# Spectral filter loaded in interleaved sets of 32 partitions, with another column order of the row tables

## The chip, the cores and the metric

The kernel runs on one core of one Trainium2 chip. The metric is the device time of one launch in microseconds (us). The kernel before takes 358.42 us, the median of three runs that lie between 358.37 and 358.54 us. Its profiled execution spans 357.2 us, and all positions in time below are counted from the start of that span.

## The reference

The program is a forward pass and its gradients. `x` is 2048 x 448 in bfloat16.

```python
def _A_ref(x, w_r, w_i):                      # spectral mixer
    X = rfft2(x.astype(float32), axes=(-2, -1))   # 2048 x 225 complex
    X = X * (w_r + 1j * w_i)
    return irfft2(X, s=(S, D)).astype(bfloat16)

h  = x + _A_ref(layernorm(x), A_w_r, A_w_i)
h2 = h + _B_ref(layernorm(h), w1, b1, w2, b2)  # layernorm, matmul, gelu, matmul over the 2048 axis
_out, _vjp = jax.vjp(f, A_x, A_w_r, A_w_i, B_w1, B_b1, B_w2, B_b2)
return (_out, *_vjp(grad_out))
```

The filter `w_r + i*w_i` has 2048 rows of 225 numbers in each of its two components; a component is 900 KB. It is read once, for the forward product, and its gradient has the same shape and is written as two outputs. What the change touches is only how the filter comes in, in which order its rows lie on the 128 partitions, and how its gradient goes out.

## The kernel before, in words

The 2048-point Fourier transform along the sequence is split into two stages, 128 = 16 x 8 by way of 16-point and 128-point parts. In the *row phase* (the loop `for t in range(NT)` at line 905) TensorE makes the 448-point transforms of the rows and the first stage: `row_a`, `row_b`. Each `row_b` pair ends in a 226 KB transfer from SBUF to SBUF (line 693) that writes 16 partitions of `D2`. There are eight of them. The *second stage* (`s2_stage`, line 696) multiplies all of `D2` by the row tables `Ut` and `Vt`, for 16 groups g of 128 rows each. The first of these products needs all eight transfers, since it contracts over all partitions of `D2`. Then `w_mult` on VectorE multiplies the result with the filter, and `s2_inv` starts the inverse transform. Its results leave by transfers of 113 KB (line 756), each of which writes 8 partitions of `D3`.

The tables `Ut` and `Vt` are made in `gen_UV` (line 465). Their column p decides which row of the spectrum falls on partition p. For the lower 64 partitions p = 4l+f, with l from 0 to 15 and f from 0 to 3. In the upper 64 the kernel before uses two blocks: partitions 64 to 111 for the residues 1 to 3 (stride 3) and 112 to 127 for residue 0 (contiguous). A table is written by eight instructions, each with 256 elements per partition, one per residue j and half; a running load count at build time picks ScalarE or VectorE for each.

The filter rows must lie in the same order. `w_load` (line 579) reads each component with four transfers into `W_rows` (a part of the region rB): 64 partitions, 48 partitions, and 16 partitions in two pieces. `w_place` (line 588) copies `W_rows` into `W_view_F` (region rG), 16 copies on ScalarE and VectorE, the upper half with its order of groups turned round. The copies are called from `s2_stage` from its fourth step (c2 = 3) on. The gradient of the filter leaves late in the kernel through `w_io` (line 563), eight transfers that `gx_consumer` (line 1358) starts at the steps named in `GW_AT`.

All engines that matter follow an order written out by hand: TensorE, VectorE, ScalarE and SyncE run their instructions in the order in which the program names them. Nearly all transfers are issued by SyncE on one queue (q1). Each takes the next of eight semaphores, so a transfer also waits until the one eight places before it has landed.

In the row phase SyncE issues, among others, the transfers to `D2`, the transposed loads of `B_w2` (`load_w2T`, line 292, 512 KB each) and the first component of the filter, one call of `w_loads` at each of the steps t = 9, 10, 11, 12. At the first step of the second stage the string `"TWWWWTTT"` (line 946) gives the order: one transposed load (T), the four loads of the second component (W), then the other transposed loads. The transposed loads feed `dg_gen` (line 827), a long product of 14 blocks of 16 matmuls with `B_w2`. `fill(n)` puts n of these matmuls between the steps of the other phases, so that TensorE has something to do there. In the second stage three stand after each half step. Block j of `dg_gen` can't start before its transposed load has landed, and since TensorE keeps its order, the second stage waits with it.

Of the kernel before, what the change touches and what calls it, by code (L numbers as in the profile page):

```python
# [17 lines left out]
P = 128  # L18
S = 2048
D = 448  # L20
DF = 225
# [101 lines left out]
def kernel(  # L123
# [20 lines left out]
    nc = tc.nc  # L144
# [110 lines left out]
    def col(n=1):  # L255
        i = _ci[0]
        _ci[0] += n
        assert _ci[0] <= 64
        return cols[:, i:i + n]
# [69 lines left out]
    def ftmp(off, *dims):  # L329
        n = int(np.prod(dims))  # L330
        v = tf[:, off:off + n]
        if len(dims) == 1:
            return v
        names = "abcd"[:len(dims)]
        return v.rearrange("p (" + " ".join(names) + ") -> p " + " ".join(names),
                           **{c: d for c, d in zip(names, dims)})
# [68 lines left out]
    def gp_madd(out, in0, scalar, in1):  # L405
        gp_.tensor_scalar(out=gtmp, in0=in0, scalar1=scalar, scalar2=None, op0=ALU.mult)
        gp_.tensor_tensor(out=out, in0=gtmp, in1=in1, op=ALU.add)
# [34 lines left out]
    def decode(eng):  # L442
        a4, fc, s_, c_, f_ = col(), col(), col(), col(), col()
        floor_div(eng, a4, pcolb, 64)
        gp_madd(s_, a4, -64.0, pcolb)
        floor_div(eng, fc, s_, 8)
        gp_madd(s_, fc, -8.0, s_)
        gp_madd(s_, s_, 2.0, a4)
        floor_div(eng, c_, fc, 4)
        gp_madd(f_, c_, -4.0, fc)  # L450
        return fc, s_, c_, f_
# [13 lines left out]
    def gen_UV():  # L465
        _, s_, c_, f_ = rows = decode(gp_)
        nrow = col()
        gp_madd(nrow, rows[0], 16.0, s_)
        msk, mk, k0, k1 = masks(gp_, c_, f_)
        slf = col()  # L470
        gp_.tensor_tensor(out=slf, in0=s_, in1=f_, op=ALU.mult)
        gp_.tensor_scalar(out=slf, in0=slf, scalar1=16.0, scalar2=1536.0, op0=ALU.mult, op1=ALU.add)
        ou, ov0, ov1, pu, pv = col(), col(), col(), col(), col()
        gp_madd(ou, c_, 1536.0, slf)
        gp_madd(ov0, c_, -512.0, slf)
        gp_.tensor_scalar(out=ov0, in0=ov0, scalar1=512.0, scalar2=None, op0=ALU.add)
        gp_.tensor_scalar(out=ov1, in0=ov0, scalar1=1024.0, scalar2=None, op0=ALU.add)
        for pt, o, kk in ((pu, ou, -1536.0), (pv, ov1, -512.0)):
            gp_.tensor_scalar(out=pt, in0=s_, scalar1=64.0, scalar2=kk, op0=ALU.mult, op1=ALU.add)
            gp_madd(pt, pt, mk, o)  # L480
        yield
        ve.tensor_scalar(out=permI[:], in0=krow[:, 0:P], scalar1=nrow, scalar2=None, op0=ALU.is_equal)
        ve.scalar_tensor_tensor(out=base[:, 0, :, 1], in0=fix, scalar=mk, in1=base[:, 0, :, 1], op0=ALU.mult, op1=ALU.add)
        for dst, o0, o1, pt in ((Ut, ou, ou, pu), (Vt, ov0, ov1, pv)):
            t = ftmp(1024 if dst is Ut else 2048, 16, 16, 2).bitcast(I32)
            for k, o in ((0, o0), (1, o1)):
                ve.tensor_scalar(out=t[:, :, :, k], in0=base[:, :, :, k], scalar1=s_, scalar2=o,
                                 op0=ALU.mult, op1=ALU.add)
                yield
            ve.tensor_scalar(out=t[:, 0, :, 1], in0=base[:, 0, :, 1], scalar1=s_, scalar2=pt, op0=ALU.mult, op1=ALU.add)  # L490
            ve.tensor_scalar(out=t, in0=t, scalar1=2047, scalar2=None, op0=ALU.bitwise_and)
            yield
            yield True
            comp = comp_ring.next()
            sc.activation(out=comp, in_=t.rearrange("p g l c -> p (g l c)"), func=ACT.Sin, scale=s2048, bias=half_uv)
            yield True
            cv = comp.rearrange("p (g l c) -> p g l c", g=16, l=16)
            for c, k in ((1, k0), (0, k1)):
                ve.tensor_scalar(out=cv[:, 0, :, c], in0=cv[:, 0, :, c], scalar1=k, scalar2=None, op0=ALU.mult)
            yield  # L500
            d0 = dst[:, :, 0:64].rearrange("p g (l f) -> p g l f", f=4)
            d1 = dst[:, :, 64:112].rearrange("p g (l f) -> p g l f", f=3)
            for j in range(4):
                m = msk[:, j:j + 1]
                dj = d1[:, :, :, j - 1] if j else dst[:, :, 112:128]
                for o, c in ((d0[:, :, :, j], 0), (dj, 1)):
                    if load[1] + 0.24 < load[0] + 0.38:
                        ve.tensor_scalar(out=o, in0=cv[:, :, :, c], scalar1=m, scalar2=None, op0=ALU.mult)
                    else:
                        sc.activation(out=o, in_=cv[:, :, :, c], func=ACT.Copy, scale=m)  # L510
                    yield
# [50 lines left out]

    def w_io(Wv, dr, di, store):
        for c_, d in ((0, dr), (1, di)):
            for p0, p1, g0, g1, row, dims in ((0, 64, 0, 16, 0, [[16 * DF, 4], [1, 16 * DF]]),
                                              (64, 112, 0, 16, 112, [[-DF, 48], [1, DF]]),
                                              (112, 128, 1, 16, 127, [[-DF, 15], [1, DF]]),
                                              (112, 128, 0, 1, 64, [[1, DF]])):
                sb = Wv[p0:p1, g0:g1, c_, 0:DF]
                d_ap = bass.AP(d.tensor, d.offset + row * DF, [[P * DF, 16]] + dims)  # L570
                if store:
                    nc.sync.dma_start(out=d_ap, in_=sb)
                else:
                    nc.sync.dma_start(out=sb, in_=d_ap)
                yield

    W_rows = cut(rB, 0, 2, NG, DF)

    def w_load():
        for c_, d in ((0, A_w_r), (1, A_w_i)):  # L580
            for p0, p1, j0, j1, row, dims in ((0, 64, 0, 16, 0, [[16 * DF, 4]]), (64, 112, 0, 16, 97, [[-16 * DF, 3]]),
                                              (112, 128, 0, 15, 113, []), (112, 128, 15, 16, 64, [])):
                nc.sync.dma_start(out=W_rows[p0:p1, c_, j0:j1, :],
                                  in_=bass.AP(d.tensor, d.offset + row * DF,
                                              [[P * DF, 16]] + dims + [[1, (j1 - j0) * DF]]))
                yield

    def w_place():
# [316 lines left out]
    for t in range(NT):  # L905
        if t in (1, 3):
            load_w2T()
        if t + 1 < NT:
            row_a(t + 1, Rs.pop(t + 1))
        fill(FILL_A[t])  # L910
        if 1 <= t and t + 3 < NT:
            if t + 3 in (4, 8, 12):
                while Meter.side:
                    Meter.side.pop(0)()
            Rs[t + 3] = scale_R(t + 3)
        row_b(t - 1)
        if t == NT - 1:
            row_b(t)
        if t % 2 and t < 12:
            fold_prep(xn, t // 2 + 2)  # L920
        for i in STATS.get(t, ()):
            ln_stats(xn, i, mvx)
        for _ in range(3 if t > 0 else 0):
            if next(uv, None):
                break
        if t in GROUPS:
            a, b = GROUPS[t]
            newton_gp(mvx[:, a:b, 1], rstd_x[:, a:b], slice(a, b))
        for _ in range((9, 10, 11, 12).count(t)):
            next(w_loads)  # L930
        if t in INV_S:
            gen_inv_s(INV_S[t])
        if t in (13, 13 + 1):
            gen_neg((cut(r448, NG * P, 12, P), cut(rE, 3 * NT * P, 4, P))[t - 13], Ut[:, 12 * (t - 13):12 + 4 * (t - 13), :])
        if t == 2:
            gen_RT()
        fill(FILL_B[t])
# [5 lines left out]

    def fwd_x(c2):
        if c2 == 0:
            for kind in "TWWWWTTT":
                if kind == "W":
                    next(w_loads)
                elif held_w2:
                    held_w2.pop(0)()  # L950
            cap[0] = NFB
            while held_w2:
                held_w2.pop(0)()
        if c2 == 4:
            turn_biases()
        return Xs[:, 2 * c2:2 * c2 + 2, :, :]

    def fwd_mult(c2, xc):
        return w_mult(c2, xc, W_view_F, False)

    s2_stage(fwd_x, fwd_mult, ML_F, 3, 24, True)
    drain()

# [283 lines left out]
    for t in range(NT):  # L1247
# [6 lines left out]
        pb, tmp, m1, m2, _ = ln_a(t, pdh[:, 0:D], rstd_h[:, t:t + 1], hln[:, t, :], (1.0 + LN_EPS) / D)  # L1254
# [98 lines left out]
    Meter.slack = 2.0  # L1353
    g_out = w_io(W_view_B, out_2, out_3, True)
    X_AT = {0: 2, 4: 3}
    GW_AT = (1, 3, 5, 6, 7, 9, 11, 12)

    def gx_consumer(t, py):
        if t in X_AT:
            load_xall(X_AT[t])  # L1360
        if t in GW_AT:
            next(g_out, None)
# [87 lines left out]
```

## Time and profile before

| what | value |
|---|---|
| median time | 358.42 us |
| span of the profiled execution | 357.2 us |
| TensorE matmul busy | 341.5 us (96%) |
| VectorE busy | 252.5 us (71%) |
| ScalarE busy | 213.8 us (60%) |
| transfers on queue q1 | 80.83 MB, 94.7% of 16 engines' span |
| first component issued / landed | 35.61 to 38.67 us / 46.15 us |
| second component issued / landed | 49.55 to 51.90 us / 57.73 us |
| last transfer to D2 issued / landed | 46.63 / 50.01 us |
| transposed load behind the second component, issued / landed | 52.00 / 60.61 us |

Busy time is the sum of an engine's instructions. The chain of work that ended last is followed back from the last instruction to whatever released it, so it tells which engine or transfer held up the end. A transfer's landing is the last of its completion marks: the trace keeps a mark for each DMA engine that finishes its part, and the landing times above are read from those marks.

### The profile page before, as it was taken

The page shows a single profiled execution, that of the slowest core. Times are in us where ns is not written, and L with a number is a line of the kernel's source. Part 1 is how long each engine was busy: PE and PEld are TensorE (multiplying, and loading weights), DVE is VectorE, ACT ScalarE, POOL GpSimd, SP SyncE. Part 2 cuts the span into 40 slices and gives each one's busy share as a digit, 9 for nine tenths or more (in the row PEclk, how much of TensorE's full clock was granted, in tenths as well). Part 3 has the DMA queues.
Part 4 walks back from the last instruction along what each step waited for, and adds up shares of the span by engine and source line. Part 5 has one row for each costly group of instructions (what it writes and reads, how often), then busy time and mean ns, then how long its engine had stood idle before and what let it go on. Part 6 is the DMA issues. An engine that isn't in the chain of part 4 may idle for free.

```text
span 357.2 us, 6450 instructions
## 1 busy us (share of the span) xinstructions
PE 341.5 (96%) x2133; PEld 183.8 (51%) x2133; DVE 252.5 (71%) x679; ACT 213.8 (60%) x457; POOL 67.7 (19%) x227
## 2 busy tenths in 40 slices
PE   6898998899999999999999999999999999999994
PEld 2455665555645555555555555544444444455641
DVE  5897626992884888775226978784498766499994
ACT  4669836965986545504221355565477776588883
POOL 8667000000220000001001111110000000056771
PEclk9699999999999999999999999999999999999998
DMA  8999999847999999997886999999976878999996
GB/s 207 287 200 234 200 198 162 169 140 252 280 292 336 302 348 241 252 246 218 194 192 134 192 210 194 221 175 264 264 214 201 238 196 236 245 215 221 247 286 234
DMA packets 147672, 81.62 MB, mean 229 GB/s; under 512 B 95480, under 2 KB 139768, under 8 KB 147384
## 3 DMA queue, kind: packets, MB, share of 16 engines
q1 hardware_dynamic: 147352, 80.83, 94.7%
q8 instruction: 16, 0.26, 0.3%
q10 hardware_dynamic: 288, 0.39, 0.3%
q14 instruction: 16, 0.13, 0.1%
HBM read 27.56 MB, written 23.89 MB: 144 GB/s over the span
## 4 chain that ended last, share of the span: by engine, by line
PE 79%; ACT 7%; DVE 6%; DMA 4%; issue 2%; SPq 1%; POOL 0%; ACTq 0%; DVEq 0%
PE ps_mm L218 66%; PE ps_ff L218 13%; DMA rO<-in_B_w_dram 2%; ACT rO L82 2%; DVE stats L82 2%; ACT rG L82 1%; DMA rA<-in_A_x_dram 1%; DVE r L82 1%; ACT Ut L82 1%; DVE rA L82 1%; DVE rS L82 1%; SPq L297 1%; ACT Vt L82 1%; ACT rX L82 0%; ACT rS L82 0%
## 5 line engine op out<-in xcount | busy, mean ns | idle before, releaser
L218 PEld LDWEIGHTS <-r 128*128 128x128 bf16 (+2 forms) x660 | 61.7, 104 | 49.6 <-issue 2.7
L218 PEld LDWEIGHTS <-rS 128*128 128x128 bf16 (+2 forms) x496 | 40.5, 99 | 38.3 <-issue 7.0
L218 PE MATMUL ps_mm<-rD,r 128*128 128x448 bf16 x224 | 44.5, 352 | 0.0
L82 ACT CAST rO<-ps_mm 128x512 bf16<-128x512 f32 (+1 forms) x62 | 33.5, 583 | 13.8 <-PE ps_mm L218 11.1
L218 PE MATMUL ps_mm<-rC,rE 128*128 128x448 bf16 x144 | 36.0, 369 | 3.3 <-DMA rC<-in_grad_out_dram 3.3
L218 PEld LDWEIGHTS <-rst 128*128 128x128 bf16 (+1 forms) x320 | 23.8, 97 | 29.3 <-issue 13.5
L82 ACT CAST r<-ps_ff 128x452 bf16<-128x452 f32 x58 | 33.4, 576 | 8.8 <-PE ps_ff L218 8.4
L218 PE MATMUL ps_mm<-r,rst 128*128 128x512 bf16 (+3 forms) x192 | 36.4, 353 | 0.0
L218 PE MATMUL ps_mm<-rB,r 128*128 128x448 bf16 x160 | 31.2, 352 | 0.1
L218 PE MATMUL ps_mm<-rG,rst 128*128 128x512 bf16 (+1 forms) x128 | 28.2, 380 | 0.0
L82 ACT ACTIVATE r<-ps_mm,rstd_h 128x448 bf16<-128x448 f32 x16 | 10.1, 633 | 26.1 <-PE ps_mm L218 26.1
L82 ACT ACTIVATE r<-rC 128x448 bf16<-128x448 bf16 x16 | 9.1, 572 | 26.8 <-DMA out_dram<-r 12.9
L82 DVE SCALAR_TENSOR_TENSOR r<-ps_mm,b2col,r 128x448 bf16<-128x448 f32 x16 | 10.9, 682 | 19.9 <-PE ps_mm L218 17.9
L82 DVE CAST rO<-ps_mm 128x512 bf16<-128x512 f32 (+1 forms) x18 | 11.8, 658 | 15.2 <-PE ps_mm L218 14.3
L82 ACT ACTIVATE rG<-rG 128x896 bf16<-128x896 bf16 x14 | 13.3, 950 | 14.9 <-DVE rG L82 14.6
L218 PEld LDWEIGHTS <-rO 128*128 128x128 bf16 (+1 forms) x165 | 15.6, 98 | 12.2 <-DMA rO<-in_B_w_dram 1.8
L218 PE MATMUL ps_mm<-rE,rS 128*128 128x448 bf16 x112 | 21.5, 352 | 0.0
L82 ACT CAST rG<-ps_mm 128x512 bf16<-128x512 f32 (+1 forms) x33 | 16.6, 541 | 7.3 <-PE ps_mm L218 7.2
L1180 POOL TENSOR_SCALAR lcol<-lcol 128x1 f32<-128x1 f32 x16 | 8.5, 530 | 65.1 <-ACT r L82 65.1
L218 PE MATMUL ps_mm<-rC,rO 128*128 128x448 bf16 x80 | 19.1, 352 | 1.5 <-DMA rO<-in_B_w_dram 1.5
L1371 POOL TENSOR_SCALAR lcol<-lcol 128x1 f32<-128x1 f32 x16 | 5.5, 342 | 78.5 <-ACT r L82 78.5
L218 PEld LDWEIGHTS <-rE 128*128 128x128 bf16 x148 | 14.4, 101 | 11.3 <-issue 5.0
(198 smaller groups left out, 662.6 us busy)
## 6 DMA issues: line engine op xcount, KB each, us to landing
out_dram<-rO SPq DMA_DIRECT2D x34, 256.0 KB
r<-in_B_w_dram SPq DMA_DIRECT2D x5, 1024.0 KB
r<-r SPq DMA_DIRECT2D x16, 226.0 KB
r<-r SPq DMA_DIRECT2D x32, 113.0 KB
rS<-in_B_w_dram SPq DMA_DIRECT2D x4, 896.0 KB
out_dram<-rG SPq DMA_DIRECT2D x10, 256.0 KB
rO<-in_B_w_dram SPq DMA_DIRECT2D x2, 1024.0 KB
w_d<-rG SPq DMA_DIRECT2D x1, 1808.0 KB
```

The source lines that it names most:

```text
L82: fn(**kw)
L218: nc.tensor.matmul(out, lhsT=lhsT, rhs=rhs, start=start, stop=stop)
L297: nc.sync.dma_start_transpose(out=wT, in_=B_w2[j * P:(j + 1) * P, :].rearrange("f (t c) -> f t c", c=P))
L1180: gp_.tensor_scalar(out=m1, in0=ms, scalar1=-1.0 / D, scalar2=None, op0=ALU.mult)
L1371: gp_.tensor_scalar(out=m1, in0=ms, scalar1=-2.0 / D, scalar2=None, op0=ALU.mult)
```

## The change

Each component of the filter now comes in with five transfers in place of four: for each residue b one that takes the partitions b, b+4, b+8, ..., 32 of them, half of them below 64 and half above; residue 0 is cut in two, since its upper rows are shifted by one group. The aim is that a transfer writes into both halves of the partitions. For this the upper half of the tables and of the filter must have the same interleaving as the lower half, p = 64+4l+j, which changes the columns of `Ut` and `Vt` and the row lists of the gradient's store: six transfers per component there, since three sets of 16 partitions take the place of one of 48. The loads of the first component are called at t = 9 (two), 10, 11 and 12, and the second component has five Ws in its string. The twelve stores start at steps 1 to 12.

```diff
@@ gen_UV
             d0 = dst[:, :, 0:64].rearrange("p g (l f) -> p g l f", f=4)
-            d1 = dst[:, :, 64:112].rearrange("p g (l f) -> p g l f", f=3)
+            d1 = dst[:, :, 64:P].rearrange("p g (l f) -> p g l f", f=4)
             for j in range(4):
                 m = msk[:, j:j + 1]
-                dj = d1[:, :, :, j - 1] if j else dst[:, :, 112:128]
-                for o, c in ((d0[:, :, :, j], 0), (dj, 1)):
+                for o, c in ((d0[:, :, :, j], 0), (d1[:, :, :, j], 1)):
@@ w_io
-            for p0, p1, g0, g1, row, dims in ((0, 64, 0, 16, 0, [[16 * DF, 4], [1, 16 * DF]]),
-                                              (64, 112, 0, 16, 112, [[-DF, 48], [1, DF]]),
-                                              (112, 128, 1, 16, 127, [[-DF, 15], [1, DF]]),
-                                              (112, 128, 0, 1, 64, [[1, DF]])):
-                sb = Wv[p0:p1, g0:g1, c_, 0:DF]
+            for sl, g0, g1, row, dims in ((slice(0, 64), 0, 16, 0, [[16 * DF, 4], [1, 16 * DF]]),
+                                          (slice(65, P, 4), 0, 16, 112, [[-DF, 16], [1, DF]]),
+                                          (slice(66, P, 4), 0, 16, 96, [[-DF, 16], [1, DF]]),
+                                          (slice(67, P, 4), 0, 16, 80, [[-DF, 16], [1, DF]]),
+                                          (slice(64, P, 4), 1, 16, 127, [[-DF, 15], [1, DF]]),
+                                          (slice(64, P, 4), 0, 1, 64, [[1, DF]])):
+                sb = Wv[sl, g0:g1, c_, 0:DF]
@@ w_load
-            for p0, p1, j0, j1, row, dims in ((0, 64, 0, 16, 0, [[16 * DF, 4]]), (64, 112, 0, 16, 97, [[-16 * DF, 3]]),
-                                              (112, 128, 0, 15, 113, []), (112, 128, 15, 16, 64, [])):
-                nc.sync.dma_start(out=W_rows[p0:p1, c_, j0:j1, :],
+            for b, j0, j1, row, up in ((0, 0, 15, 0, 113), (0, 15, 16, 15, 49), (1, 0, 16, 16, 81), (2, 0, 16, 32, 49), (3, 0, 16, 48, 17)):
+                nc.sync.dma_start(out=W_rows[b:P:4, c_, j0:j1, :],
                                   in_=bass.AP(d.tensor, d.offset + row * DF,
-                                              [[P * DF, 16]] + dims + [[1, (j1 - j0) * DF]]))
+                                              [[up * DF, 2], [P * DF, 16], [1, (j1 - j0) * DF]]))
@@ row phase, fwd_x, the gradient's store
-        for _ in range((9, 10, 11, 12).count(t)):
+        for _ in range((9, 9, 10, 11, 12).count(t)):
-            for kind in "TWWWWTTT":
+            for kind in "TWWWWWTTT":
-    GW_AT = (1, 3, 5, 6, 7, 9, 11, 12)
+    GW_AT = (1, 2, 3, 4, 5, 6, 7, 8, 9, 10, 11, 12)
```

## The prediction

> **What bounds the kernel now.** I read the page first: what ended last, by engine and line.
>
> ```profile
> PE 79%; ACT 7%; DVE 6%; DMA 4%; issue 2%; SPq 1%; POOL 0%; ACTq 0%; DVEq 0%
> PE ps_mm L218 66%; PE ps_ff L218 13%; DMA rO<-in_B_w_dram 2%; ACT rO L82 2%; DVE stats L82 2%; ACT rG L82 1%; DMA rA<-in_A_x_dram 1%; DVE r L82 1%; ACT Ut L82 1%; DVE rA L82 1%; DVE rS L82 1%; SPq L297 1%; ACT Vt L82 1%; ACT rX L82 0%; ACT rS L82 0%
> ```
>
> TensorE sets the end, so a change counts only where it lengthens or shortens a wait of TensorE. One transfer has 2% of the chain: a transposed load of `B_w2` into rO. The chain between 44 and 64 us shows where.
>
> ```profile
> 45.90 4.35 PE ps_mm L218 x23
> ...
> 52.00 8.60 DMA rO<-in_B_w_dram
> 60.61 0.05 issue
> 60.65 0.55 PE ps_mm L218 x2
> ```
>
> That load is issued at 52.00 and lands at 60.61. Next I took SyncE's order of issue (start, duration, line) to see what stands ahead of it.
>
> ```profile
> 35.61 1.28 SPq L583 DMA_DIRECT2D rB<-in_A_w_r_dram  x2
> ...
> 49.55 2.35 SPq L583 DMA_DIRECT2D rB<-in_A_w_i_dram  x4
> 52.00 5.02 SPq L297 DMA_TRANSPOSE rO<-in_B_w_dram  x1
> ```
>
> Directly ahead of it is the filter's second component (L583). Last, TensorE and VectorE in that stretch:
>
> ```profile
> 50.31 0.35 PE L218 MATMUL ps_ff<-r,Vt 128*128 128x452 bf16 x1
> ...
> 60.65 0.55 PE L218 MATMUL ps_mm<-rC,rO 128*128 128x448 bf16 x2 [1.50 <-DMA rO<-in_B_w_dram]
> ```
> ```profile
> 57.72 2.89 DVE L82 COPY rG<-rB 64x900 bf16<-64x900 bf16 x7
> ```
>
> The second stage begins at 50.31, 0.3 us after the last transfer to D2 lands (50.01). TensorE waits 1.50 us for the transposed load. The filter lands at 57.73, when VectorE copies it. So what delays D2 delays TensorE, the transposed load is late already, and the filter comes just in time. All three run on one queue, q1.
>
> [...] While the 64-partition load runs, 39.50 to 41.50 us, the core moves 194 GB/s; the 128-partition store at 86.50 to 90.00 gives 355 GB/s. In the packet records, rows of 7200 B take a median of 568 ns in the loads of before and 271 ns at their quickest. [...] transfers that write 16 partitions of D2 (source 128) leave 16 landing marks, those that write 8 partitions of D3 (source 128) leave 9, which I read as 8 engines and one mark for the rest; those with 14 rows on both sides leave 15. No transfer of before has the small size on the source alone. [...]
>
> **The change part by part.** *Loads.* Before, the filter's outermost sizes are 64, 48 or 16 on the SBUF side and 16 in memory[...]. Now they are 32 and **2** (the list begins with `[up * DF, 2]`)[...]. Engines 0 and 1 carry the whole filter and the other 14 none of it. This is what I build on. Each of the two then moves 16 rows per transfer. [...] I take the quickest packet, 271 ns for 7200 B (26.6 GB/s; the 3584 B packets of other loads make 25.6 GB/s with all engines busy). Per component: three transfers of 16 rows, 48 x 0.271 = 13.0 us; 16 rows of 6750 B, by size, 16 x 0.254 = 4.1 us; 16 rows of 450 B at 26 ns, 0.4 us. Sum 17.5 us on engines 0 and 1, against 5.8 us before (landings 51.95 to 57.73).
>
> What queues behind: in the changed program SyncE issues, after the transfer to D2 that lands at 39.27, three of the first component's loads, a transfer to D2, the other two loads, three transfers to D2, a transposed load, the five loads of the second component, and the load the chain waits for. None passes another on engines 0 and 1. A transfer to D2 takes 8 packets of 1808 B, 75 ns each, 0.6 us; a transposed load 128 packets of 256 B, 18 ns each, 2.3 us. So:
> - last transfer to D2: 39.3 + 17.5 + 4 x 0.6 = 59.2 us, before 50.01. TensorE, in order, has nothing else and idles from 50.3: 9 us.
> - second component: 59.2 + 2.3 + 17.5 = 79.0 us, before 57.73. TensorE reaches the fourth step near 68; there VectorE meets the copy of the second component and stands until 79.0, with everything queued behind it (PSUM evacuations, then the filter product).
> - the transposed load behind it: 79.0 + 2.3 = 81.3 us, before 60.61. TensorE can go on 20.7 us later than before. The first idle time is inside this, not on top.
>
> After 81.3 the later transposed loads come 2.3 us apart, as before, and all else hangs on TensorE: the lost time isn't given back. D3 transfers, loads of `B_w1` and so on shift as a whole.
>
> *Clock.* [...] The trace shows such a stretch at the start of the kernel (columns: stretch, length, busy time with count for PE, PEld, DVE, ACT and POOL, clock, DMA share, GB/s):
>
> ```profile
> 8.00:12.00 4.00, 2.53 (x12) 1.33 (x12) 2.80 (x9) 1.38 (x2) 3.28 (x17) 0.73 1.03 347
> 12.00:16.00 4.00, 3.72 (x14) 1.32 (x13) 2.98 (x12) 3.08 (x8) 2.70 (x12) 0.50 1.22 244
> ```
>
> The first recovery is hidden in the second wait. [...] TensorE waits 0.95 us for ScalarE at 68.6 anyway, so I take 1.2, with 0 and 2.0 as ends.
>
> *Tables.* The one contiguous table write per table takes 468 and 462 ns on ScalarE, strided ones up to 884: at most 2 x 0.4 us more. It lies ahead of the D2 transfers, and is hidden by the queue of engines 0 and 1: 0. *Store.* Same bytes, same 450 B packets, outermost sizes 16 on both sides[...]; four more issues of about 0.6 us on SyncE between 311 and 345 us, while TensorE runs to 352.2: 0, at most 0.5.
>
> **Sum:** 358.4 + 20.7 + 1.2 = 380.3 us. I round to 380.5 for the gaps between transfers.
>
> **The rivals.** *A, all 16 engines carry the loads*[...]. Then a component takes 6 x 0.271 + 2 x 0.254 + 0.05 = 2.2 us, not 5.8, the transposed load lands some 3 us earlier, and TensorE's 1.50 us goes away; 0.5 us comes back from the tables and the extra issues: 357.4 us. [...] *B, both effects small:* 16 engines, but the wait is taken over by ScalarE's copies of the filter (rG, 1% of the chain) and the strided tables: 358.5 us. Speaks against it that the wait on the load is 1.50 us and tables cost 0.8 at most. *C, two engines, but each at the pace of the loads of before,* 568 ns per row: 48 x 0.568 + 16 x 0.53 + 0.4 = 36 us per component, the last load at 39.3 + 72 + 2.4 + 4.6 = 118 us, 58 us late: 418 us. For it: the median packet. [...] Within the main case, the pace of a packet may be 10% off (3.5 us); if other transfers could pass the filter, engines 0 and 1 would still need 35 us from 39.3 on, the filter would land at 75 at the earliest and the result be near 375.
>
> **How the numbers follow.** Main case 0.84, A 0.08, B 0.03, C 0.05. Predicted time 380.5. Low end 373: the case in which transfers pass, less clock loss. High end 388: packets 10% slower, a full 2 us of clock, gaps of 0.2 us between transfers. A, B and C stay outside the range, together 0.16. Faster 0.08, same 0.03, slower 0.89.
>
> **What would show it.** Filter loads leave 3 landing marks each (2 engines and the rest), not 16; they land about 4.4 us apart; last D2 transfer near 59, second component near 79, transposed load near 81; in the page, TensorE's and the clock's digits fall between 50 and 82 us with the DMA share at two sixteenths, and the chain gives some 30 us to transfers. From 90 to the end all as before, 22 us later. If the loads have 16 marks, A or B holds and the forecast is wrong; if they land over 8 us apart, C.

## The result, and the profile after

The changed kernel takes 385.91 us (385.02 to 387.53, three runs) against 358.42: 1.0773 times, interval 1.0716 to 1.083. The forecast was 380.5 us in a range of 373 to 388. The profiled execution spans 383.3 us, 26.1 more than before.

TensorE's instructions and their order are the same, and so are the bytes. In the 40 slices of the page (9.6 us each; PEclk is the clock that TensorE was granted, in tenths) TensorE has a hole in the sixth to ninth slice, and its clock is low in the seventh and the ninth. The smaller dip in the fourth slice, 3.4 us at half the clock from 30.68 us on, lies ahead of both waits; the profile of run 4 has it too, without them.

```profile
PE   6898956419999999999999999999999999999994
...
PEclk9698996958999999999999999999999999999999
DMA  8999299167479999999968698997998569999984
```

TensorE's timeline shows that the hole is two waits (in brackets: idle time before the instruction, and what ended it):

```profile
60.69 0.56 PE L218 MATMUL ps_ff<-r,Vt 128*128 128x452 bf16 x1 [7.93 <-DMA r<-r]
...
84.64 0.93 PE L218 MATMUL ps_mm<-rC,rO 128*128 128x448 bf16 x2 [13.25 <-DMA rO<-in_B_w_dram]
```

The first is for the last transfer to D2; before, the same matmul ran at 50.31 with no wait. The second is for the transposed load, which cost 1.50 us before. VectorE stood in that time too, at the copy of the filter:

```profile
81.40 2.90 DVE L82 COPY rG<-rB 64x900 bf16<-64x900 bf16 x7 [11.31 <-DMA rB<-in_A_w_i_dram]
```

Why the transfers were late is in the load of the 16 DMA engines from 50 to 82 us, in 40 slices of 0.8 us: their mean busy share in tenths, then GB/s.

```profile
DMA  7991111111111990111391111111111111111129
GB/s 160 273 124 54 45 54 54 54 54 52 47 48 31 251 255 0 25 42 51 100 152 44 61 54 54 54 54 54 54 45 54 54 54 54 45 54 54 54 53 289
```

Busy 0.1, or 54 GB/s: two engines of 16, each at 27. The marks of the other transfers show the queue on these two directly: of the transfer to D2 issued at 38.49, behind three loads of the filter, 14 marks come at 40.97 to 41.56 us and the other two at 49.43 and 49.95.

SyncE stood as well (start, duration, line):

```profile
49.53 10.93 SPq L297 DMA_TRANSPOSE rO<-in_B_w_dram  x1
60.52 3.14 SPq L583 DMA_DIRECT2D rB<-in_A_w_i_dram  x5
63.76 17.35 SPq L297 DMA_TRANSPOSE rO<-in_B_w_dram  x1
```

A transposed load whose issue took 5.02 us before holds SyncE for 10.93 and 17.35 us. Each of these issues ends just before the last transfer in front of it lands (60.46 and 60.64 us, 81.11 and 81.28); what holds them, the trace doesn't show. The landings:

| landing (us) | before | after | forecast |
|---|---|---|---|
| marks of a filter load | 16 | 3 | 3 |
| last transfer to D2 | 50.01 | 60.64 | 59.2 |
| second component, last load | 57.73 | 81.28 | 79.0 |
| transposed load behind it | 60.61 | 84.59 | 81.3 |
| first matmul of the inverse rows | 87.72 | 113.74 | |

The page's chain is of little use here: its shares sum to 73%, and followed back from the end it breaks off at 96.57 us, before it gets to either wait. Where a chain stops short, TensorE's timeline with its idle times does the work.

### The profile page after: what moved, and what is told of

It is laid out like the page before. It is cut to its first block, busy times and chain, and to the rows that moved or that the text cites. A ratio compares the mean times of both kernels' runs of the same rounds, so it can differ in the third digit from the quotient of the medians.

```text
span 383.3 us, 6458 instructions
## 1 busy us (share of the span) xinstructions
PE 347.4 (91%) x2133; PEld 185.8 (48%) x2133; DVE 253.0 (66%) x679; ACT 215.1 (56%) x457; POOL 67.0 (17%) x227
## 4 chain that ended last, share of the span: by engine, by line
PE 68%; ACT 2%; DVE 2%; issue 1%; POOL 0%; ACTq 0%; DVEq 0%
PE ps_mm L218 58%; PE ps_ff L218 10%; ACT rO L82 2%; DVE rA L82 1%; DVE r L82 0%; DVE rS L82 0%; ACT rAT L82 0%; DVE rB L82 0%; POOL lcol L1180 0%; ACT rD L82 0%; ACT r L82 0%; ACT rstd_h L82 0%; ACT rG L82 0%; POOL nmean_h L986 0%; DVE rstd_h L82 0%
## 5 line engine op out<-in xcount | busy, mean ns | idle before, releaser
L218 PE MATMUL ps_mm<-rC,rE 128*128 128x448 bf16 x144 | 37.3, 379 | 3.3 <-DMA rC<-in_grad_out_dram 3.3
L82 ACT CAST r<-ps_ff 128x452 bf16<-128x452 f32 x58 | 33.3, 575 | 11.3 <-PE ps_ff L218 10.4
L218 PE MATMUL ps_mm<-rC,rO 128*128 128x448 bf16 x80 | 21.6, 388 | 13.3 <-DMA rO<-in_B_w_dram 13.3
L82 ACT ACTIVATE r<-ps_mm,rstd_h 128x448 bf16<-128x448 f32 x16 | 10.1, 633 | 26.1 <-PE ps_mm L218 26.1
L1180 POOL TENSOR_SCALAR lcol<-lcol 128x1 f32<-128x1 f32 x16 | 8.5, 532 | 65.1 <-ACT r L82 65.1
L218 PE MATMUL ps_ff<-csI,rAT 113*128 113x224 bf16 (+1 forms) x108 | 19.0, 298 | 0.6 <-ACT rAT L82 0.4
```

Source lines behind the costliest of these rows:

```text
L82: fn(**kw)
L218: nc.tensor.matmul(out, lhsT=lhsT, rhs=rhs, start=start, stop=stop)
L1180: gp_.tensor_scalar(out=m1, in0=ms, scalar1=-1.0 / D, scalar2=None, op0=ALU.mult)
```

## The experiments

All ratios are to the kernel before on the same chip.

**1. Sixteen engines for the same sets.** Each load is cut into its two halves, so that the outermost size is 16.

```diff
-nc.sync.dma_start(out=W_rows[b:P:4, c_, j0:j1, :],
-                  in_=bass.AP(d.tensor, d.offset + row * DF, [[up * DF, 2], [P * DF, 16], [1, (j1 - j0) * DF]]))
+for hf in range(2):
+    nc.sync.dma_start(out=W_rows[64 * hf + b:64 * hf + 64:4, c_, j0:j1, :],
+                      in_=bass.AP(d.tensor, d.offset + (row + hf * up) * DF, [[P * DF, 16], [1, (j1 - j0) * DF]]))
```

> The changed kernel, but each filter load is cut into its lower and its upper 16 partitions, so that the outermost size in memory is 16 and not 2. Layout, tables, order and the store stay as changed. My theory (two engines carry the load): 16 landing marks per load, a component lands within about 6 us as in the kernel before, both long waits of TensorE go, time 358.5 us (357.5 to 360). Rival (the layout costs: partitions in steps of 4, strided table columns, the store in twelve parts): the time stays above 375 us.

Measured: 361.62 us, 1.0071 (1.0044 to 1.0099). 16 marks per load; the wait for D2 is 0.2 us, that for the transposed load as follows.

```profile
PE ps_mm L218 <- DMA rO<-in_B_w_dram: 2.7, 1, 2.7
```

24.3 us of the 27.5 are gone; columns, tables, placement and store are still those of the change, and only the loads differ: 16 engines in place of two, and twice as many transfers, each into one half. The time is above what I expected: the second component is now ten transfers, and issuing them takes SyncE from 50.20 to 56.47 us, so that the transposed load is issued at 56.56 (before 52.00) and lands at 62.41. TensorE's wait is 1.2 us longer than before, and from 61.80 us on its clock is at half for 3.4 us: the stretch from the wait to the inverse rows takes 28.58 us, in the kernel before 27.07. Run 4 tests whether the layout costs anything.

**2 and 3. One component each.** The load with outermost size 2 for the first component only, and for the second only; the other comes in halves.

```diff
-for hf in range(2): ...
+if c_ == 0: ...      # run 3: c_ == 1
+    [[up * DF, 2], [P * DF, 16], [1, (j1 - j0) * DF]]
+else: ...
+    for hf in range(2): ...
```

> Only the first component (w_r) by the changed loads with outermost size 2; the second by halves of 16 partitions. If the two waits add up in the queue: last transfer to D2 lands near 60.6 us, TensorE waits about 8 us in front of the second stage, the transposed load behind the second component lands near 72.5, time about 371 us. If one component alone makes the whole loss (the waits overlap): 358 to 360 or 385 us.

> Only the second component (w_i) by the changed loads with outermost size 2; the first by halves. If the two waits add up: D2 lands near 50 us and TensorE does not wait there; the second component lands near 70, the transposed load behind it near 73, TensorE waits about 13 us once, time about 372 us. With the run of the first component alone, the two losses sum to the 27.5 us of the change. If the waits overlap: about 385 us.

Measured: first component alone 370.04 us, 1.0311 (1.0255 to 1.0367); second alone 375.78 us, 1.0471 (1.0393 to 1.0549). TensorE's waits for transfers, of the first and then the second run:

```profile
PE ps_ff L218 <- DMA r<-r: 9.0, 1, 9.0
PE ps_mm L218 <- DMA rO<-in_B_w_dram: 1.7, 1, 1.7
```
```profile
PE ps_mm L218 <- DMA rO<-in_B_w_dram: 14.5, 1, 14.5
```

Each component makes its own wait, and within the spread of the runs they add: over run 1, which has neither, the two losses are 8.4 and 14.2 us, together 22.6, against 24.3 for both in the changed kernel. The last transfer to D2 landed at 59.96 and 49.94 us, the transposed load at 72.33 and 73.83. The second run is 3.8 us above its expectation; its two timed runs lie 3.5 us apart (374.03, the profiled one, and 377.53), so I read no more into it than that the waits add.

**4. The layout with few issues.** The lower 64 partitions in one transfer, the upper half in five of 16 partitions; tables, `w_place` and store as changed. (Left out below: one more call at t = 10 and one more W.)

```diff
-for b, j0, j1, row, up in (...):
+for sl, j0, j1, row, dims in ((slice(0, 64), 0, 16, 0, [[16 * DF, 4]]), (slice(65, P, 4), 0, 16, 97, []),
+                              (slice(66, P, 4), 0, 16, 81, []), (slice(67, P, 4), 0, 16, 65, []),
+                              (slice(64, P, 4), 0, 15, 113, []), (slice(64, P, 4), 15, 16, 64, [])):
```

> The changed kernel's column order, tables, filter placement and store, but the filter loaded with 16 engines in few pieces: the lower 64 partitions in one transfer, the upper half in five of 16 partitions (outermost size in memory 16 in all). If the layout itself costs nothing and the 2.9 us left by the halves came from issuing ten transfers per component: the second component and the transposed load behind it land within 1 us of the kernel before (57.7 and 60.6 us), time 358.8 us (358.2 to 360). If tables, store or strided partitions cost: 361 us or more, with the loss outside the stretch from 44 to 65 us.

Measured: 358.54 us against 359.45 for the kernel before on that chip, 0.9972 (0.9959 to 0.9984). So column order, strided tables, placement and the twelve stores together cost nothing that shows, and this version beats both kernels by a little; a small cost could be hidden behind its quicker loads. The second component lands 4.8 us after the load in front of it (53.49 to 58.33; before 5.8), the transposed load at 59.88, and TensorE doesn't wait for it. The one profile doesn't show where the 0.28% come from, and that stays open: it is of the slowest of the 22 timed runs (360.06 us), with the clock at half for 3.4 us from 29.86 on, and its second stage begins at 52.09 us, 1.8 us later than before.

**5 and 6. Fewer engines in the kernel before.** The 64- and 48-partition loads cut along l into two (four) transfers, with outermost size 8 (4).

```diff
+n = 2 if p0 < 112 else 1          # 4 in the second
+for q in range(n):
+    s, e = p0 + q * (p1 - p0) // n, p0 + (q + 1) * (p1 - p0) // n
+    ... W_rows[s:e, ...], offset (row + 16 // n * q * P) * DF, [[P * DF, 16 // n]] + dims + ...
```

> The kernel before, its 64- and 48-partition filter loads cut into two transfers each with outermost size 8 in memory: eight engines[...], the same bytes to the same partitions. If [...] an engine alone is quick: 7200-byte packets take about 271 ns and not 568, a component takes as long as before (within 1 us), time 358.5 us (357.5 to 359.5). If the number of engines sets the rate at any count: component some 10 us, time 364 to 368 us.

> The same with four transfers each, outermost size 4: four engines. Per component 28 packets of 7200 bytes per engine, 7.6 us, and the 16-partition pieces 1 us: 8.6 us against 5.8, so each component is about 2.9 us longer, and the loss is 3 to 6 us: time 363 us (361 to 365). [...]

Measured: eight engines 362.09 us, 1.0075 (1.0049 to 1.01); four engines 367.99 us, 1.0237 (1.0204 to 1.0271). Marks per load 9 and 5. The packets' medians are 275 and 273 ns against 568, as expected, and for the lower half the reckoning holds: its 450 KB land 2.12 and 2.89 us (first and second component) after the transfer in front of them on eight engines, 2.36 and 2.63 us on sixteen. So half of the engines carry the lower half as fast as all of them. For the upper half the reckoning does not hold: its pieces of 168 KB on eight engines, three rows each, land 2.1 and 1.4 us apart in the second component where 0.8 was expected, and 84 KB on four engines 1.0 to 1.4. The reason was not tested. The next transfer, which writes to the upper half too, is under way by then: on eight engines the first marks of the 6750-byte piece come at 56.16 us, the last of the pieces in front of it at 59.08. So a component takes 6.8 us (eight) and 10.4 us (four) from the landing in front of it, not 5.8 and 8.6, and both times are above what I expected. TensorE waits 2.6 us for the transposed load with eight engines; with four it waits 3.2 us for D2 and 4.7 us for the load, and the clock falls at both (its mean over the profiled execution is 0.979, with eight engines 0.989). The order of 16, 8, 4 and 2 engines (the last in the changed kernel) is 1, 1.0075, 1.0237 and 1.0773; the number of transfers per component differs as well (4, 6, 10 and 5).

**7 and 8. TensorE kept busy in the waits.** Extra matmuls, read by nobody, in front of the second stage and of the wait for the transposed load, first 38 and 64, then 48 and 80 narrower ones; with them the changed kernel once more, on the same chip as the second (the first was on another).

```diff
+def keep_busy(n):
+    pt = ps_mm()
+    for _ in range(n):
+        nc.tensor.matmul(pt[:, 0:D], lhsT=ident[:], rhs=go_tp[:, 0, :], start=True, stop=True)
...
+if make_inv and g == 0: keep_busy(38)
...
+if make_inv and c2 == 3 and i == 1: keep_busy(64)
```

> The changed kernel with 38 extra matmuls in front of the second stage and 64 in front of the wait for the transposed load, whose results nobody reads, so that TensorE is busy in both waits. If half the clock after a wait costs 1 us at the end: clock 1.00 just after the second wait, stretch after it 8.0 instead of 8.9 us, time 384.8 us (384 to 385.3). If the clock costs nothing (the work behind is bound by ScalarE and VectorE): 385.9 us. If the extra matmuls delay the rest: over 386.5 us.

> The changed kernel with 48 and 80 extra matmuls of 350 columns in its two long waits, their results read by nobody: 256 instructions on TensorE more, so that the 16 KB instruction packet should fall at the same place of the work as in the changed kernel (82.5 us, in front of the last mark of the transposed load). If half the clock alone costs what the stretches show (8.9 against 8.0 us, and 0.7 us later): transposed load lands near 84.5 as in the changed kernel, clock 1.00 behind it, 1 to 1.7 us less than the changed kernel on the same chip. If the 3.3 us of the first run with extra matmuls were all clock: 3 us less. If they were all the packet: no difference.

> The changed kernel unaltered, on the same chip as the run with extra matmuls, as its yardstick: 385.9 us (384.5 to 388), ratio 1.077 to before.

Measured: 382.6 us, 1.067 (1.0625 to 1.0715), 2.2 us below what I expected; 385.84 us, 1.0746 (1.0718 to 1.0774); unaltered 385.14 us, 1.0716 (1.0686 to 1.0747). The stretch from the end of the second wait to the first matmul of the inverse rows does the same work in all. Columns as in the prediction, the clock third from the end; kernel before, unaltered changed kernel, first and second run with extra matmuls:

```profile
60.65:87.72 27.07, 25.84 (x164) 15.24 (x165) 18.02 (x39) 19.69 (x35) 1.01 (x2) 1.00 0.69 179
```
```profile
84.29:113.39 29.10, 28.27 (x164) 15.57 (x165) 18.03 (x39) 19.80 (x35) 0.41 (x2) 0.94 0.63 166
```
```profile
83.20:110.63 27.43, 25.98 (x164) 15.17 (x165) 18.87 (x42) 19.69 (x35) 0.73 (x2) 1.00 0.76 181
```
```profile
84.23:113.35 29.12, 28.74 (x165) 16.11 (x165) 18.03 (x39) 19.78 (x35) 0.59 (x2) 0.90 0.66 166
```

With the clock at 1.00 the stretch takes 27.43 us, without 29.10, and the difference lies in TensorE's busy time (25.98 and 28.27): the clock costs 1.7 us. The second run failed in its purpose. Its 80 matmuls end at 80.81, TensorE still waits 3.24 us, and the clock falls all the same (0.51 from 85 to 90 us), so it repeats the changed kernel instead of separating the clock from the other part. That other part is the landing of the transposed load: 83.15 us in the first run, 84.24 unaltered, 84.19 in the second. In the first run alone the 16 KB packet of the instruction queue lies elsewhere (63.13 and 86.25 us; in the other two at 82.16 and 82.01), and there the load's marks lie within 0.4 us of each other, against 1.6 and 1.7. So of the 2.76 us by which the first run reaches the inverse rows earlier than the unaltered one, 1.7 are the clock and 1.1 go with the place of that packet.

**9. The packet in the kernel before.** Four warm-up matmuls in place of twelve.

```diff
-for _ in range(12):
+for _ in range(4):
     nc.tensor.matmul(idle[:, 0:D], ...)
```

> The kernel before with 4 warm-up matmuls at its start in place of 12 (their result is read by nobody), so that TensorE's program is 16 instructions shorter. The transposed load that TensorE waits for has its first mark at 59.22 and its last at 60.61 us, while one engine carries a 16 KB packet of the instruction queue from 58.75 us on for 0.95 us. If that fetch is what makes the last mark late: the packet moves by about 1.5 us, the marks lie within 0.5 us, the wait of 1.5 us shrinks to 0.3 and the time to 357.2 us. If the fetch has nothing to do with it, or doesn't move: 358.5 us.

Measured: 359.02 us, 0.9991 (0.9975 to 1.0006). The packet moved, from 58.75 to 62.47 us (3.7 us and not 1.5), the load's marks lie at 59.27 to 59.80, and the wait shrank from 1.5 to 0.5 us, nearly as expected; the time didn't follow. What is gained there is given back later, or the packets that moved cost elsewhere. Which, the run doesn't tell.

**10 and 11. The other half on another queue.** The kernel before, the upper half of the second component issued by GpSimd, then by ScalarE.

```diff
-nc.sync.dma_start(out=W_rows[p0:p1, c_, j0:j1, :],
+(nc.gpsimd if c_ and p0 else nc.sync).dma_start(out=W_rows[p0:p1, c_, j0:j1, :],   # then nc.scalar
```

> The kernel before, with the upper half of the second component (three of its four loads) issued by GpSimd on a queue of its own; nothing else differs, and in GpSimd's order they come early, near the start. [...] both halves in flight or out of the way shorten the queue in front of the transposed load by about 3 us: it lands near 57.5 and not 60.61, TensorE's 1.5 us wait goes: 357.3 us. If 450 KB more among the first loads of the kernel delay the first rows instead, 359 to 361 us.

> The kernel before, with the upper half of the second component issued by ScalarE on its own queue at the start of the second stage, at the place where SyncE issues the lower half. [...] the second component lands near 55.5 and not 57.73, the transposed load near 58, the 1.5 us wait goes: 357.3 us. If ScalarE's three issues (1.4 us, and their waits for landings) delay the copies that TensorE waits for: 359 to 361 us.

Measured: GpSimd 360.54 us, 1.0036 (1.0024 to 1.0049); ScalarE 359.31 us, 1.0017 (0.9999 to 1.0034). No gain by either. On GpSimd the wait for the transposed load is gone, as expected (it lands at 59.03 us). But the upper half goes at 6 to 8.8 us, among the first loads, and TensorE pays at once, with 5.09 us where it waited 2.21 at most before:

```profile
11.58 2.65 PE L218 MATMUL ps_mm<-rC,rE 128*128 128x448 bf16 x6 [5.09 <-DMA rC<-in_grad_out_dram]
```

From ScalarE the upper half runs from 50.8 us on, ahead of the lower half, not beside it: the last of its large packets starts at 52.53 us, the lower half's first at 53.11. The lower half's packets stay at a median of 590 ns, and TensorE still waits 2.0 us for the transposed load. Two halves at once were not achieved in these two runs, and no run loads both halves with one transfer on 16 engines. So whether the aim of the change would pay was not tried, and that writing both halves at once is quicker was not shown.

## Why the prediction was right, and where its sizes were off

- **Two engines.** Right, and it is the cause: three marks, 54 GB/s, and run 1 takes 24.3 of the 27.5 us away with outermost size 16, at the cost of more transfers. That a small size in memory alone would do this was my estimate: in the kernel before fewer marks were seen only with a small size at the destination (9 for the transfers to D3) or on both sides. Now sizes of 2, 4 and 8 in memory alone leave 3, 5 and 9 marks. Which two of the 16 engines carry the filter (0 and 1 in the forecast), no trace shows.
- **The pace of an engine.** Right: median 273 ns for 7200 B, forecast 271. Rival C (568 ns) falls.
- **Queueing.** Right in kind: D2, the filter and the transposed load follow each other on the two engines, and runs 2 and 3 show that the two delays add. The size was 3.3 us short: "79.0 + 2.3 = 81.3 us" measured 84.59. The terms that were too small: 1.4 us up to D2 (59.2 against 60.64), on the way to which one of the two engines falls up to 1.0 us behind the other (marks of the third load 48.59 and 49.63); about 1.3 us for the first load of the second component, which landed 5.3 us after the load in front of it, not 4.1. I had put the transfers end to end, but SyncE stood in the transposed load until 60.46, issued the filter after that, and its first two packets took 1.05 and 1.58 us. And 1.0 us for the transposed load (3.3 us in place of 2.3), with the instruction packet on one engine. The transposed load in between took 0.5 us less than I gave it (1.8 in place of 2.3).
- **The clock.** Right in kind, and 1.7 us in the run that removes it, against the 1.2 I took (ends 0 and 2.0), which was my estimate. It came back at 88.71 us, 4.1 us after the end of the wait. One long wait isn't needed for a fall: in the kernel before, my own example, the clock falls at 9.81 us though no wait of TensorE is longer than 2.21 us. The last section has the figures.
- **Tables and store at nothing.** Right. The contiguous writes of 468 and 462 ns became strided ones of about 825, ScalarE's table writes sum to 9.3 us where 8.3 stood (VectorE's, which I had left out, to 2.5 where 2.2 stood), and run 4 shows no loss with both in.
- **Nothing given back.** Right: 24.0 us late at the transposed load, 26.0 at the inverse rows, 26.1 at the end.
- **Rivals A and B** needed 16 engines, and fall. Run 4 gains 0.28%, about the 1 us of 358.4 (0.3%) that A gave, and in its profile the wait that A named is gone. But its transfers write one half each, and TensorE comes to that place later than before, so I don't count it for A. A itself, a transfer into both halves on 16 engines, was not run.
- **What would show it.** One sign failed: the chain was to give some 30 us to transfers, but it breaks off after the waits and gives them none.

In sum 20.7 + 1.2 was forecast; the profile has 24.0 + 2.0. All the terms of the queue but one were too small. The medians differ by 27.5 us and the two profiles by 26.1; the rest is the spread of the runs.

## What to carry to other kernels

Before a transfer's access pattern is rearranged to reach more of SBUF, look at the outermost size on both sides: with a leading dimension of 2 in memory alone, two engines carried 1.8 MB at 54 GB/s. Then ask what is queued behind: TensorE's two waits, 7.93 and 13.25 us, ended with a transfer to D2 and a transposed load that stood behind the filter on the same two engines. (The filter itself was little earlier: VectorE stood for it until 81.40 us.) Count the landing marks of one transfer, too: here the filter loads that moved 54 GB/s, at a busy share of 0.13 of the 16 engines, left 3 marks; 5, 9 and 16 marks I read as 4, 8 and 16 engines.

## What was not expected of the hardware

- A transposed load held SyncE, which issued it, for 10.93 and 17.35 us while the filter's packets were still queued on two engines, and all later transfers were issued after that.
- In eight of the fourteen traces (two kernels, twelve runs) a 16 KB packet of the instruction queue, 0.95 to 1.18 us on one DMA engine, starts about 2 us before the awaited transposed load lands. There the last of the load's 16 marks comes 1.4 to 1.7 us after the first. In five traces in which the packet lies elsewhere, all marks lie within 0.53 us. (In run 5 the packet meets the load too, and the marks lie within 0.23 us.) With eight of TensorE's matmuls left out, in run 9, the packet moved.
- Eight engines load the lower 64 partitions as fast as sixteen (2.12 and 2.89 us for 450 KB, against 2.36 and 2.63).
- The length of a wait alone didn't decide here whether TensorE's clock fell: with 2.67 us in run 1 it fell (0.68 from 60 to 65 us), with 2.60 us in run 5 and 2.25 us in run 8 it didn't (1.00 from 60 to 65 us in run 8), and in the kernel before it fell at 9.81 us with no wait over 2.21. In the traces of the kernel before and the changed kernel the clock changes only at moments that lie whole multiples of 3.41 us apart. Cut both traces into stretches of 3.41 us on this grid, and take the share of each in which TensorE was busy with matmuls (as the profile models their ends). The clock went from full to half after seven stretches, whose shares are 0 to 0.458, and stayed full after the other 194, whose shares are 0.467 to 1. It came back after five, with shares of 0.995 to 1, and not after six, with 0 to 0.755. Each of the changed kernel's two long waits covers a whole stretch, from 54.58 and from 71.65 us: both have a share of 0, and the clock fell after both.
